# Moving the convolution and the transposes of block 1 one step later inside block 0

## The chip, the cores and the metric

The kernel runs on one core of a Trainium2 chip. The metric is device time in microseconds (us) of one execution. Traces come from the hardware profiler, one execution each. Engines: PE is TensorE, PEld its weight load, DVE is VectorE, ACT is ScalarE, POOL is GpSimd, SP issues DMAs.

## The reference, cut to what matters

```python
def _attn_ref(x, weight):                 # x: 8 x 4096 x 192, weight: 8 heads x 7 taps
    w = softmax(weight, axis=-1)          # (cut: written out, with 1e-9 in the sum)
    # causal convolution over the sequence, 7 taps, one set of taps for each head's 24 channels
    out = np.einsum('hk,bskhg->bshg', w, x_unf)
    return out.reshape(B, S, D)

def _moe_ref(x, w_gate, w_val, w_out):    # x: 32768 x 192, d_ff = 1536
    g = x @ w_gate
    silu = g * (1.0 / (1.0 + np.exp(-g)))
    val = x @ w_val
    return (silu * val @ w_out).astype(np.float32)
```

A short convolution feeds a gated feed-forward layer. The kernel works in blocks of 512 tokens (64 of them). A block has 12 chunks of 128 of the 1536 hidden columns, so there are 768 chunks in all, counted by `n` from 0.

## The kernel before: the parts that matter

For the first four blocks the convolution is made as small matmuls on PE (`early`), then turned by PE transposes (`eturn`; the fourth block by a DMA instead), then used by the chunks (`gate_val`). The results of PE go to banks of the memory PSUM; an eviction is the copy of a bank out of PSUM by ACT or DVE, after which the bank can be used again. A chunk is six matmuls, three pairs on the two row halves of the array. `slot(1, 0)` is the first accumulation of the output of block 0.

```python
# order of the loads on POOL's queue, at the start
xe_load(0)
...
load_w(0)                     # first two thirds of the gate and value weights
load_w(1)
xe_tile(1)
xe_load(1)                    # rows of block 1: two loads, one for each row half
load_w(2)                     # last third of the weights, needed from chunk 8 on
for m in range(3):
    load_wo(m)
...

def early(e, where):          # conv of block e: 64 small matmuls into three PSUM banks
    ...                       # moving operand: xe[e]
    # evictions: ACT (bank 0), DVE (bank 2), ACT (bank 1), then a DVE duplicate inside tme[e]

def eturn(b, where):          # transposes of block b: 3 x 5, each three into its own bank
    for k in range(SL):
        pool, tag = where[k]
        bank = pool.tile([P, EG, P], fp16, tag=tag, name="turn")
        ...                   # five PE transposes of tme[b] into bank
        (dve, act, dve)[k](...)    # eviction to xc: DVE, ACT, DVE

def gate_val(n):
    g = ppool.tile([P, TB], fp32, tag="gate", name="gate")    # three buffers each
    v = ppool.tile([P, TB], fp32, tag="val", name="val")
    ...                       # 3 pairs of matmuls
    silu[n] = seq(nc.scalar.activation(sg, g, AF.Silu)).ins
    seq(nc.vector.tensor_tensor(hj, sg, v, op=ALU.mult))      # the product of chunk n
    ...

acc_banks = (apool, "acc0"), (apool, "acc1")   # one buffer each: conv, transposes and
                                               # the accumulation share them
for n in range(n_steps):
    ...
    gate_val(n)
    if n == 5:
        early(1, (*acc_banks, gate_bank))
    elif n == 7:
        eturn(1, (*acc_banks, gate_bank))
    elif n in (9, 12, 15, 17):
        k = {9: 1, 12: 2, 15: 3, 17: 4}[n]
        slot(k, 0, silu[n - 1 if k == 4 else n - 2], work)
    ...
```

`seq` fixes the order of each engine's instructions as the program states it. The accumulation needs both accumulator banks, and the two row halves write both of them in turn, so it needs both of them empty.

Of the kernel before, what the change touches and what calls it, by code (L numbers as in the profile page):

```python
# [10 lines left out]
def kernel(  # L11
# [113 lines left out]
    def x16_tile(u):  # L125
        x16[u] = cpool.tile([P, 4 * NG, D], fp16, tag="x16", name="x16")
# [16 lines left out]
    def dup_x(u, queue=None):  # L143
        for r in range(2):
            p0 = Q * r
            seq(
                (queue or nc.sync).dma_start(
                    out=x16[u][p0 + 32 : p0 + 64], in_=x16[u][p0 : p0 + 32]
                )
            )  # L150
# [250 lines left out]
    def eout(e):  # L401
        scre[e] = dpool.tile([XW, 4 * Q], fp16, tag="scre", name="scre")
        rows = scre[e].rearrange("(g c j) d -> c j g d", c=2, j=EO)
        for c in range(2):
            seq(
                nc.sync.dma_start(
                    out=rows[c], in_=tme[e][Q * c : Q * c + EO, :, :]
                )
            )

    def efetch(b):
        xc[b] = []
        for k in range(SL):
            t = cpool.tile([P, XW], fp16, tag=f"xc{k}", name=f"xc{k}", bufs=6)
            seq(
                nc.sync.dma_start_transpose(
                    out=t[:, 0:TB], in_=scre[b][0:TB, Q * k : Q * k + P]
                )
            )
            xc[b].append(t)  # L420

    def eturn(b, where):
        xc[b] = []
        for k in range(SL):
            t = cpool.tile([P, XW], fp16, tag=f"xc{k}", name=f"xc{k}", bufs=6)
            pool, tag = where[k]
            bank = pool.tile([P, EG, P], fp16, tag=tag, name="turn")
            for g in range(EG):
                seq(
                    nc.tensor.transpose(  # L430
                        bank[:, g, :], tme[b][:, g, Q * k : Q * k + P], ident
                    )
                )
            seq(
                (dve, act, dve)[k](
                    t.rearrange("p (g c j) -> p g c j", c=2, j=EO),
                    bank.rearrange("p g (c q) -> p g c q", c=2)[:, :, :, 0:EO],
                )
            )
            xc[b].append(t)  # L440
# [47 lines left out]
    def conv_dup(u):  # L488
        seq(nc.gpsimd.tensor_copy(tm[u][:, :, SL * Q : 4 * Q], tm[u][:, :, 0:Q]))  # L489

    def conv_out(u, m):
        r, c = divmod(m, 4)
        t0 = NG * CO * m
        full = min(NG, (UT - t0) // CO)
        rest = min(UT - t0 - full * CO, CO) if full < NG else 0
        seq(
            nc.sync.dma_start(
                out=scr[u][t0 : t0 + full * CO, :].rearrange("(g j) d -> j g d", j=CO),
                in_=tm[u][32 * c : 32 * c + CO, NG * r : NG * r + full, :],
            )  # L500
        )
        if rest:
            t1 = t0 + full * CO
            seq(
                nc.sync.dma_start(
                    out=scr[u][t1 : t1 + rest, :],
                    in_=tm[u][32 * c : 32 * c + rest, NG * r + full, :],
                )
            )
# [3 lines left out]
    def fetch(b):  # L513
        u, i = divmod(b, UB)
        xc[b] = []
        for k in range(SL):
            t = cpool.tile([P, XW], fp16, tag=f"xc{k}", name=f"xc{k}", bufs=6)
            seq(
                nc.sync.dma_start_transpose(
                    out=t[:, 0:TB], in_=scr[u][TB * i : TB * i + TB, Q * k : Q * k + P]  # L520
                )
            )
            xc[b].append(t)
# [5 lines left out]
    def gate_val(n):  # L529
        b, j = divmod(n, NCH)  # L530
        g = ppool.tile([P, TB], fp32, tag="gate", name="gate")
        v = ppool.tile([P, TB], fp32, tag="val", name="val")
        m, e = divmod(j, E)
        for k in range(SL):
            for half, o in ((0, g), (1, v)):
                p0 = Q * half
                seq(
                    nc.tensor.matmul(  # L538
                        o,
                        w16[m][p0 : p0 + Q, k, e::E],  # L540
                        xc[b][k][p0 : p0 + Q, 0:TB],
                        start=(k == 0),
                        stop=(k == SL - 1),
                    )
                )
        sg = hpool.tile([P, TB], fp16, tag="sig", name="sig", bufs=3)
        silu[n] = seq(nc.scalar.activation(sg, g, AF.Silu)).ins  # L547
        hj = hpool.tile([P, TB], fp16, tag="h", name="h", bufs=15)
        seq(nc.vector.tensor_tensor(hj, sg, v, op=ALU.mult))  # L549
        hbuf[n] = hj  # L550
# [46 lines left out]
    def slot(k, b, after=None, between=None):  # L597

        if k == 1:
            acc[b] = [  # L600
                apool.tile([P, 2, D], fp32, tag=f"acc{i}", name=f"acc{i}")
                for i in range(2)
            ]
            down(b, [(False, G[0])], 1, after)
            if between is not None:
                between()
            down(b, [(False, G[1])], 1, None)
        elif k == 2:
            down(b, [(True, G[0]), (True, G[1])], 0, after)
            if between is not None:  # L610
                between()
            if b < n_blocks - 1:
                down(b, [(False, G[2])], 0, None)
        elif k == 3:
            down(b, [(True, G[2])], 1, after)
            if between is not None:
                between()
            down(b, [(False, G[3])], 1, None)
        else:
            down(b, [(True, G[3])], 0, after)  # L620
            o_sb = hpool.tile([P, SUBS, D], fp32, tag="o_sb", name="o_sb", bufs=3)
            seq(nc.scalar.copy(o_sb[:, 0:2, :], acc[b][0]))  # L622
            seq(nc.vector.tensor_copy(o_sb[:, 2:4, :], acc[b][1]))  # L623
            t0 = b * TB
            seq(
                nc.sync.dma_start(
                    out=out[t0 : t0 + TB, :].rearrange("(s p) d -> p s d", p=P),
                    in_=o_sb,
                )
            )  # L630
            del acc[b]
# [25 lines left out]
    for n in range(n_steps):  # L657
        b, j = divmod(n, NCH)
        u, ls = divmod(n, ustep)
        work = None  # L660
        if n in (12, 19):

            def work(e=2 if n == 12 else 3):
                early(e, (gate_bank, gate_bank, val_bank))

        at = (25, 31) if u == 0 else (10, 22)
        if u + 1 < NU and ls in at:

            def work(u=u, hh=at.index(ls)):
                conv_half(u + 1, hh)  # L670

        gate_val(n)
        if n == 5:
            early(1, (*acc_banks, gate_bank))
        elif n == 7:
            eturn(1, (*acc_banks, gate_bank))
        elif n in (9, 12, 15, 17):
            k = {9: 1, 12: 2, 15: 3, 17: 4}[n]
            slot(k, 0, silu[n - 1 if k == 4 else n - 2], work)
        elif j % 3 == 1 and n > 18:  # L680
            k = {1: 3, 4: 4, 7: 1, 10: 2}[j]
            slot(k, b - 1 if j < 7 else b, silu[n - 2], work)
        if n == 18:
            eturn(2, (*acc_banks, gate_bank))
        elif n == 20:
            eout(3)
        elif n == 21:
            efetch(3)
        if u + 1 < NU:
            if ls == at[0]:  # L690
                conv_dup(u + 1)
            if ls == at[1]:
                for m in range(2):
                    conv_out(u + 1, m)
            if ls == at[1] + 1:
                for m in range(2, 8):
                    conv_out(u + 1, m)
            lo = 32 if u == 0 else 28
            if ls in range(lo, lo + 12, 3):
                fetch(UB * (u + 1) + (ls - lo) // 3)  # L700
        if u + 2 < NU:
            if ls == (21 if u == 0 else 1):
                x16_tile(u + 2)
                load_x(u + 2, 0, silu[n - 1])
            if ls == (23 if u == 0 else 5):
                load_x(u + 2, 1, silu[n - 1])
            if ls == (37 if u == 0 else 26):
                dup_x(u + 2)
# [42 lines left out]
```

## Time and profile before

The median of three runs was 791.72 us (791.31 to 791.74). These are lines of the page of the kernel before: busy time of TensorE with its share of the span and its instructions, then the shares of the chain of work that ended last.

```profile
span 789.7 us, 28564 instructions
...
PE 782.5 (99%) x12007; PEld 526.3 (67%) x12007; DVE 583.0 (74%) x928; ACT 522.1 (66%) x910; POOL 67.6 (9%) x95
...
PE 97%; POOL 1%; DMA 1%; DVE 0%; ACT 0%; issue 0%; POOLq 0%
```

The chain of work is PE nearly everywhere, and the change removes no instruction, so it can only win time in which PE stands still. The DMA share of that chain (1%) is one load, `xe<-in_x_dram`. These are lines of the timeline of PE and of VectorE in the kernel before, from 12 to 20 us: start, length, engine, source line, operation, tiles, number of instructions, and in brackets idle time before with what ended it.

```profile
13.56 1.03 PE L372 MATMUL cv<-xe,wide 64*64 64x72 f16 x64 [0.43 <-DMA xe<-in_x_dram]
15.94 1.01 PE L430 MATMUL turn<-ident,tme 128*128 128x128 f16 x15
18.20 1.15 PE L564 MATMUL acc<-wo,h 64*128 64x192 f16 x24
...
16.02 1.34 DVE L549 TENSOR_TENSOR h<-sig,val 128x512 f16<-128x512 f16 x2 [0.22 <-PE val L538]
17.27 0.76 DVE L435 COPY xc<-turn 128x520 f16<-128x520 f16 x2
```

The three PE lines are the conv of block 1, its transposes and the first accumulation. The conv's first matmul is held by one load, and 63 of its matmuls are held by the other, which landed at 13.82 us. VectorE had emptied the first accumulator bank at 17.70, half a microsecond before the accumulation began at 18.20. The waits of the same kernel between 8 and 24 us (who waited for what: us in total, times, longest) name the load:

```profile
PEld L372 <- DMA xe<-in_x_dram: 0.7, 1, 0.7
...
PE cv L372 <- DMA xe<-in_x_dram: 0.4, 1, 0.4
```

### The profile page before, as it was taken

Reading aid. Unit: us, or ns where it says so; the run is one execution under the profiler, and the core shown is the slowest. Engines: PE = TensorE matmul, PEld = TensorE weight load, DVE = VectorE, ACT = ScalarE, POOL = GpSimd, SP = SyncE. Lnnn points to the kernel's source line nnn. Section 1 sums busy time; section 2 is a strip of 40 time slices with the busy share of each in tenths; the row PEclk is TensorE's granted clock in tenths of the full one; section 3 lists DMA queues with packets and bytes.
Section 4 is the critical chain, followed back from the end, with each engine's and each line's share of the span. In section 5 each row is a group of like instructions: output and inputs, shape, how many; then the busy total and the mean of one; then the engine's idle time right before and its main releaser. Section 6 shows DMA issues by size and latency. Waiting matters only on the chain.

```text
span 789.7 us, 28564 instructions
## 1 busy us (share of the span) xinstructions
PE 782.5 (99%) x12007; PEld 526.3 (67%) x12007; DVE 583.0 (74%) x928; ACT 522.1 (66%) x910; POOL 67.6 (9%) x95
## 2 busy tenths in 40 slices
PE   8999999999999999999999999999999999999997
PEld 4666666666666666666666666666666666666665
DVE  7677777777777777868777777777777777777775
ACT  6676666676666666666667666666667667676664
POOL 8201010010100101001010000100001010000000
PEclk9999999999999999999999999999999999999999
DMA  9999875797757868469794758857579784725311
GB/s 142 155 151 160 174 110 114 155 119 151 103 126 143 132 145 138 105 129 119 151 145 119 119 110 163 126 142 116 106 148 131 145 125 114 135 80 115 81 42 42
DMA packets 213825, 99.22 MB, mean 126 GB/s; under 512 B 147256, under 2 KB 212800, under 8 KB 212800
## 3 DMA queue, kind: packets, MB, share of 16 engines
q1 hardware_dynamic: 167696, 78.95, 48.2%
q0 software_dynamic: 46000, 18.45, 22.2%
q8 instruction: 94, 1.54, 0.8%
q14 instruction: 35, 0.29, 0.1%
HBM read 36.89 MB, written 41.16 MB: 99 GB/s over the span
## 4 chain that ended last, share of the span: by engine, by line
PE 97%; POOL 1%; DMA 1%; DVE 0%; ACT 0%; issue 0%; POOLq 0%
PE gate L538 61%; PE acc L564 32%; PE cv L461 2%; PE val L538 1%; DMA xe<-in_x_dram 1%; POOL w L167 0%; POOL xe L97 0%; PE acc L585 0%; PE cv L372 0%; PE turn L430 0%; DVE h L549 0%; ACT sig L547 0%; DVE o_sb L623 0%; ACT o_sb L719 0%; POOL jn L191 0%
## 5 line engine op out<-in xcount | busy, mean ns | idle before, releaser
L549 DVE TENSOR_TENSOR h<-sig,val 128x512 f16<-128x512 f16 x768 | 507.7, 688 | 194.8 <-PE val L538 191.6
L547 ACT ACTIVATE sig<-gate 128x512 f16<-128x512 f32 x768 | 458.5, 597 | 234.1 <-PE val L538 207.5
L538 PE MATMUL gate<-xc,w 64*128 64x512 f16 x2304 | 539.0, 376 | 0.0
L538 PE MATMUL val<-xc,w 64*128 64x512 f16 x2304 | 538.8, 376 | 0.1
L538 PEld LDWEIGHTS <-w 64*128 64x128 f16 x4608 | 253.7, 110 | 183.5 <-DMA w<-in_moe_w_val_dram 0.4
L564 PEld LDWEIGHTS <-h 64*128 64x128 f16 x6096 | 257.3, 94 | 62.4 <-issue 5.9
L564 PE MATMUL acc<-wo,h 64*128 64x192 f16 x6096 | 298.5, 243 | 0.0
L97 POOL DMA_DIRECT2D x<-in_x_dram x40 | 31.5, 794 | 435.8 <-ACT sig L547 427.1
L478 ACT CAST tm<-cv 128x480 f16<-128x480 f32 x60 | 30.6, 562 | 22.1 <-PE cv L461 22.1
L478 DVE CAST tm<-cv 128x480 f16<-128x480 f32 x60 | 36.6, 652 | 2.6
L623 DVE COPY o_sb<-acc 128x384 f32<-128x384 f32 x63 | 34.7, 551 | 0.0
L489 POOL COPY tm<-tm 128x1280 f16<-128x1280 f16 x15 | 18.8, 1252 | 136.3 <-DVE tm L478 128.1
L622 ACT COPY o_sb<-acc 128x384 f32<-128x384 f32 x63 | 30.2, 479 | 0.1
L461 PE MATMUL cv<-x,band 64*32 64x240 f16 x960 | 18.4, 265 | 0.0
L461 PEld LDWEIGHTS <-band 64*32 64x32 f16 x960 | 10.1, 91 | 5.0 <-issue 4.7
L132 POOL MEMSET x<- 6x192 f16 x7 | 1.7, 247 | 59.7 <-PE cv L461 59.6
L97 POOL DMA_DIRECT2D xe<-in_x_dram x9 | 6.0, 680 | 1.2 <-DMA xe<-in_x_dram 1.1
L639 PE MATMUL warm<-fill 128*128 128x512 f16 (+1 forms) x12 | 3.9, 483 | 1.0 <-DVE fill L91 1.0
L390 ACT CAST tme<-cv 128x288 f16<-128x288 f32 x8 | 2.9, 401 | 2.5 <-PE cv L372 2.5
L372 PE MATMUL cv<-xe,wide 64*64 64x48 f16 (+1 forms) x256 | 3.2, 192 | 1.1 <-ACT wide L330 0.6
L372 PEld LDWEIGHTS <-wide 64*64 64x64 f16 x256 | 2.7, 108 | 2.3 <-ACT wide L330 0.8
L430 PE MATMUL turn<-ident,tme 128*128 128x128 f16 x45 | 3.2, 220 | 0.6 <-ACT tme L390 0.5
(52 smaller groups left out, 37.2 us busy)
## 6 DMA issues: line engine op xcount, KB each, us to landing
out_dram<-o_sb SPq DMA_DIRECT2D x63, 384.0 KB
scr<-tm SPq DMA_DIRECT2D x105, 130.0 KB
x<-x SPq DMA_DIRECT2D x28, 480.0 KB
x<-in_x_dram POOLq DMA_DIRECT2D x24, 480.0 KB, 9.7
x<-in_x_dram POOLq DMA_DIRECT2D x7, 468.0 KB, 7.7
xc<-scr SPq DMA_TRANSPOSE x180
scr<-tm SPq DMA_DIRECT2D x15, 104.0 KB
w<-in_moe_w_gate_dram POOLq DMA_DIRECT2D x3, 192.0 KB, 5.3
```

Of the source, the lines that this page charges most:

```text
L97: nc.gpsimd.dma_start(out=t[p0 + i0 : p0 + i1, w0 - at : w1 - at, :], in_=bass.AP(tensor=x_flat.tensor, offset=(t0 + size * w0 - pad + i0) ...
L372: nc.tensor.matmul(o[Q * c : Q * c + Q, at : at + w], wide[Q * r : Q * r + Q, a, h, :], xe[e][Q * r : Q * r + Q, c : 2 * G : 2, h * grp : ...
L461: nc.tensor.matmul(banks[r][32 * c : 32 * c + 32, t * w : t * w + w], band[Q * r : Q * r + Q, h, :], x16[u][Q * r : Q * r + Q, NG * c : NG ...
L478: eng(tm[u][:, NG * r : NG * r + NG, 2 * grp * hp : 2 * grp * hp + 2 * grp].rearrange("p g (t e) -> p g t e", t=2), banks[r][:, 0 : 2 * w] ...
L489: seq(nc.gpsimd.tensor_copy(tm[u][:, :, SL * Q : 4 * Q], tm[u][:, :, 0:Q]))
L538: nc.tensor.matmul(o, w16[m][p0 : p0 + Q, k, e::E], xc[b][k][p0 : p0 + Q, 0:TB], start=(k == 0), stop=(k == SL - 1),)
L547: silu[n] = seq(nc.scalar.activation(sg, g, AF.Silu)).ins
L549: seq(nc.vector.tensor_tensor(hj, sg, v, op=ALU.mult))
L564: nc.tensor.matmul(acc[b][bank][:, s, :], hj[p0 : p0 + Q, ts(2 * bank + s, P)], wo16[p0 : p0 + Q, j, :], start=(not second and j == 0 and ...
L622: seq(nc.scalar.copy(o_sb[:, 0:2, :], acc[b][0]))
L623: seq(nc.vector.tensor_copy(o_sb[:, 2:4, :], acc[b][1]))
L639: nc.tensor.matmul(warm[:, 0:width], fill, fill.unsqueeze(1).to_broadcast([P, width // P, P]), start=True, stop=True, skip_group_check=True,)
```

## The change

The intent is to give the rows of block 1 one chunk (0.65 us) more to arrive, and to keep two chunks between the conv and its transposes, so that the conv's evictions have time.

```diff
         gate_val(n)
-        if n == 5:
+        if n == 6:
             early(1, (*acc_banks, gate_bank))
-        elif n == 7:
+        elif n == 8:
             eturn(1, (*acc_banks, gate_bank))
         elif n in (9, 12, 15, 17):
```

## The prediction

> **What bounds it now.** TensorE: busy 782.5 of 789.7 us on the page, and the chain of work that ended last is 97% PE. Busy time alone does not prove it (the Trainium skill, "Perfetto Trace Analysis", section "Identifying the Most-Contended Engine": matmul occupancy is not a good measure); the chain view does. So time is gained only where PE stands still, and the change touches only about 12.8 to 18.2 us.
>
> **The wait aimed at.** In the timeline the last pair of chunk 5 issues at 12.75 us (a pair takes 0.215). The conv of block 1 then waits for its input: two loads land at about 13.5 and 13.82 us, and 59 of its 64 matmuls are in the chain after 13.87. The next chunk starts at 14.52. The conv of block 2, unhindered, takes 0.66 us (22.22 to 22.89). So PE loses about 14.52 - 12.97 - 0.66 = 0.9 us.
>
> **What the change does.** No instruction is added or removed. Chunk 6 moves before the conv, chunk 8 before the transposes. Two chunks still lie between conv and transposes, but only chunk 9, not 8 and 9, between the transposes and the first accumulation of block 0. Estimates from these durations:
> 1. Chunk 6 (0.65 us) issues at 13.0 to 13.7; its banks come free at 12.93 (SiLU of chunk 3) and 13.00 (product of chunk 3). The conv starts near 13.7, waits until 13.87 for its second load, and ends at 14.52 as before. PE is one chunk, 0.65 us, ahead.
> 2. Chunks 7 and 8 issue from 14.52 to 15.85. Chunk 8 needs the last weight third, whose loads land at 14.57, 15.17 and 15.50 us: just in time.
> 3. Transposes at 15.93 to 16.85 as before; chunk 9 to about 17.55.
> 4. The accumulation wants both accumulator banks, which the transposes filled. VectorE empties the first only after its queue: product 6 (0.69, start 14.5), conv eviction (0.56), duplicate (0.45), products 7 and 8 (0.69 each), then 0.42. Estimated end 17.8 to 17.9, so PE waits 0.3 to 0.4 us there. Before, that eviction ended at 17.69 and the accumulation started at 18.20, without a wait.
>
> The Trainium skill, "TensorEngine Tiling (Array Packing)", section "PSUM Bottleneck", says tiling speeds up TensorE but not PSUM evacuation. The trace agrees here: a row-tiled chunk takes PE 0.65 us, VectorE's product 0.69.
>
> The accumulation thus starts near 17.95 instead of 18.20: of 0.65 us moved into the wait about 0.25 remains, the rest is given back at the accumulator banks. Later stages keep their order and are PE-bound.
>
> **Time.** 791.72 - 0.25 = 791.45 us; 791.0 to 791.95 should hold it 8 times in 10 (the runs before spread 0.43 us). Faster by over 2%: 0.003; within 2%: 0.994; slower: 0.003.
>
> **What the profile would show.** Right: PE's wait before the conv (timeline, waits) falls from 0.9 to at most 0.25 us; the conv's end stays near 14.5; a new PE gap of 0.2 to 0.5 us before the first accumulation, released by VectorE's eviction of the transposes; the accumulation starts at 17.8 to 18.05. Wrong: the conv ends at 13.9, no gap at the accumulation (gain 0.65), or it starts at 18.2 or later (gain zero or negative).
>
> **What would make it wrong.** Load landings that shift by some tenths: chunk 8 now meets its weights just as they land; a longer VectorE queue would take back the whole gain; run spread as large as the effect.

## The result, and the profile after

| kernel | runs | median us | lowest to highest us |
|---|---|---|---|
| before | 6 | 791.73 | 791.22 to 792.90 |
| changed | 6 | 791.55 | 791.16 to 792.59 |

The ratio is 0.9997, with a 95% interval of 0.9985 to 1.001. A ratio is the mean time of one kernel's runs over that of the other's of the same rounds, so it is not quite the ratio of the medians in the table. The interval is about 1 us to each side, so timing alone cannot show an effect of a few tenths; the traces have to.

These are the same timeline lines in the changed kernel.

```profile
14.05 0.73 PE L372 MATMUL cv<-xe,wide 64*64 64x72 f16 x64
16.13 1.01 PE L430 MATMUL turn<-ident,tme 128*128 128x128 f16 x15
17.75 1.34 PE L564 MATMUL acc<-wo,h 64*128 64x192 f16 x24
...
16.21 1.33 DVE L549 TENSOR_TENSOR h<-sig,val 128x512 f16<-128x512 f16 x2
17.46 0.76 DVE L435 COPY xc<-turn 128x520 f16<-128x520 f16 x2
```

The conv has no wait for its load. The accumulation begins 0.46 us earlier, but its 24 matmuls take 1.34 us instead of 1.15: the first is at 17.75, the second at 17.94, just after VectorE finished emptying the bank at 17.89. That is a pause of 0.19 us, which the kernel before does not have.

Taken chunk by chunk (start of each chunk's SiLU in the two traces), the changed kernel is 0.27 us earlier at chunk 13 and still 0.27 us earlier at chunk 767. So nothing after the first block takes up or adds to the difference of these two traces. But the first chunk was 0.25 us *later* in the changed kernel's trace, before the two programs differ at all. So the start-up has a draw of its own, and two traces are not enough.

### The profile page after: what moved, and what is told of

Same layout as the page of the kernel before. It is cut to its first block, busy times and chain, and to the rows that moved or that the text cites. A ratio compares the mean times of both kernels' runs of the same rounds, so it can differ in the third digit from the quotient of the medians. Undisturbed runs are those within 1.5% of the kernel's fastest.

```text
span 789.5 us, 28564 instructions
## 1 busy us (share of the span) xinstructions
PE 782.9 (99%) x12007; PEld 527.2 (67%) x12007; DVE 582.9 (74%) x928; ACT 522.1 (66%) x910; POOL 67.5 (9%) x95
## 4 chain that ended last, share of the span: by engine, by line
PE 99%; ACT 0%; DVE 0%; issue 0%
PE gate L538 62%; PE acc L564 32%; PE cv L461 2%; PE val L538 1%; PE warm L639 1%; PE turn L430 0%; PE cv L372 0%; PE acc L585 0%; ACT tme L390 0%; DVE h L549 0%; ACT wide L330 0%; ACT sig L547 0%; DVE o_sb L623 0%; ACT o_sb L719 0%; PE taps L317 0%
## 5 line engine op out<-in xcount | busy, mean ns | idle before, releaser
L430 PEld LDWEIGHTS <-tme 128*128 128x128 f16 x45 | 2.6, 97 | 1.8 <-issue 1.1
```

Of the source, the lines that this page charges most:

```text
L430: nc.tensor.transpose(bank[:, g, :], tme[b][:, g, Q * k : Q * k + P], ident)
```

## The experiments

Theory: the change removes up to one chunk (0.65 us) of a wait for the load of block 1's rows, whatever that wait is in a given run, and gives back a fixed pause at the accumulator banks, because only one chunk now lies between the transposes and the accumulation. Rivals: the difference of the two traces is chance at start-up; VectorE is the limit in this stage, so that time won at the load is lost to it; or the pause has another cause than the order of VectorE's work.

For each trace the table gives the start of the first chunk's SiLU (PE's own start-up), the landing of the second load of block 1's rows, the wait that the conv had for it (the time from the chunk before the conv to the chunk after it, less 0.215 us for the last pair, 0.66 for the conv and 0.09 that every trace has), the time from the first matmul of the chunk after the conv to the SiLU of chunk 13, and that from the SiLU of chunk 13 to that of chunk 767. All are read from single instructions of the traces, in us.

| trace | conv / transposes behind chunk | first SiLU | load lands | wait | after conv to chunk 13 | chunk 13 to 767 |
|---|---|---|---|---|---|---|
| before | 5 / 7 | 9.66 | 13.82 | 0.81 | 9.71 | 758.99 |
| rep_before | 5 / 7 | 10.13 | 13.64 | 0.15 | 9.71 | 759.37 |
| rep_before2 | 5 / 7 | 9.91 | 14.08 | 0.81 | 9.72 | 758.98 |
| before_nowait | 5 / 7 | 10.53 | 12.34, not used | 0 | 9.71 | 758.98 |
| before_late | 5 / 7 | 10.52 | 15.25 | 1.37 | 9.72 | 758.99 |
| changed | 6 / 8 | 9.91 | 13.93 | 0 | 9.25 | 758.99 |
| rep_after | 6 / 8 | 9.92 | 13.28 | 0 | 9.26 | 759.03 |
| rep_after2 | 6 / 8 | 9.91 | 13.31 | 0 | 9.26 | 758.98 |
| after_nowait | 6 / 8 | 9.73 | 13.77, not used | 0 | 9.25 | 759.01 |
| after_late | 6 / 8 | 9.96 | 15.69 | 1.63 | 9.25 | 759.91 |
| turn_only | 5 / 8 | 10.53 | 13.13 | 0 | 9.90 | 759.24 |
| conv_only | 6 / 7 | 9.69 | 13.18 | 0 | 9.23 | 760.60 |
| after_bank | 6 / 8 | 9.92 | 15.12 | 1.00 | 9.07 | 758.99 |
| after_first | 6 / 8 | 9.93 | 13.67 | 0 | 9.07 | 759.78 |

With the conv behind chunk 6 one chunk less is left to do after it. A chunk is three pairs of 0.2155 us, 0.65 us. If nothing were given back, the sixth column would read 9.71 - 0.65 = 9.06 to 9.07 us for these orders. The difference from that is the give-back.

### rep_before: the kernel before again

Edit: none.

> The kernel before again, unchanged, for a second trace of it. Main theory (PE loses about 0.9 us before the conv of block 1, to a load): the conv again waits for its second load, which lands at 13.8 give or take 0.2 us, whatever PE's own start-up does; first accumulation at 18.2 (18.0 to 18.4), without a wait for a bank. Rival (the 0.27 us between the two traces is the chance of two start-ups): the accumulation of this trace differs from the first trace of the same kernel by as much as 0.3 us.

The load landed at 13.64 and the accumulation began at 18.02, without a pause. But the conv waited only 0.15 us for it instead of 0.81, since PE had started 0.47 us later. Chunk 13 was 0.18 us earlier than in the first trace of the same program. So the theory's intervals hold, and the rival is right that single traces of one program differ by about as much as the effect.

### rep_after: the changed kernel again, timed

Edit: none beyond the change.

> The changed kernel again, unchanged. Main theory: conv ends at 14.5 to 14.75, its wait for the load is at most 0.2 us; first accumulation matmul at 17.55 to 17.8 and the second 0.1 to 0.3 us after it, when VectorE has emptied the bank; everything from chunk 13 on is 0.25 to 0.45 us earlier than in the kernel before, by the same amount to the end. Rival (chance): the shift is anywhere between -0.3 and +0.3. The timed ratio should be 0.9990 to 1.0005, too coarse to tell the two apart; the traces decide.

Accumulation at 17.76, its second matmul at 17.95: the pause repeats. The time after the conv repeats to 0.01 us. The shift at chunk 13 is -0.26 us against the first trace of the kernel before, but only -0.08 against rep_before: the expected 0.25 to 0.45 us does not hold for every pair. Timed: 791.45 us median (791.02 to 792.91, 6 runs) against 791.76 for the kernel before (11 runs), ratio 0.9997, 0.9985 to 1.0009.

### before_nowait: the old order without the load

```diff
-                                xe[e][
+                                xe[0 if e == 1 else e][
```

The result is wrong: block 1 is computed from block 0's rows.

> The kernel before, with the conv of block 1 reading the rows of block 0 (wrong result on purpose), which are there long before, so that it never waits for its load. Main theory: the conv ends at 13.6 to 13.9 and the whole 0.9 us is kept, since two chunks still lie between transposes and accumulation: first accumulation at 17.3 to 17.6, chunk 13 and all after 0.7 to 0.9 us earlier than in the kernel before. Rival (VectorE's queue is the limit here, and PE only waits elsewhere when the load comes early): accumulation at 17.8 or later with a wait for VectorE, gain 0.3 us or less.

The forecast of absolute times failed: the accumulation began at 18.27. The reason lies in the start-up, not at the conv: the first SiLU was at 10.53, 0.87 us later than in the first trace. The load landed at 12.34 here, so even the unedited kernel would not have waited in this execution. What this trace can still tell is the other half of the theory: the time from the conv to chunk 13 is 9.71 us as in the traces that waited, so time that is not spent on the wait is not lost to VectorE later in this order.

What drew the later start can be read in the timeline of the first microseconds. The first fence is the kernel before, the second before_nowait; the lines are PE's warming matmuls (eight, then four narrower ones) and the four matmuls that spread the taps.

```profile
1.00 3.28 PE L639 MATMUL warm<-fill 128*128 128x512 f16 x8 [1.00 <-DVE fill L91]
4.35 0.61 PE L639 MATMUL warm<-fill 128*128 128x256 f16 x4
5.01 0.60 PE L317 MATMUL taps<-spread,shift 128*128 128x256 f16 x4
```

```profile
1.00 3.59 PE L639 MATMUL warm<-fill 128*128 128x512 f16 x8 [1.00 <-DVE fill L91]
4.67 1.03 PE L639 MATMUL warm<-fill 128*128 128x256 f16 x4
5.50 1.06 PE L317 MATMUL taps<-spread,shift 128*128 128x256 f16 x4
```

The same four tap matmuls, whose inputs were ready in both, take 0.60 us in one and 1.06 in the other. Single ones took 269 to 272 ns against 421. The Trainium skill, "TensorE: Matmul & The Clock Gate", section "What's actually happening", says that PE starts at a slow clock and is let go after a busy window that runs freely, and that "the transition point varies ±500ns". The traces agree that the point varies, but it varies by more than that. PE's first matmul is at 1.00 us in all of them. In the first trace the matmuls turned fast during the seventh warming matmul, which ended at 4.07 us; in before_nowait the last tap matmul, begun at 6.14, was still slow. So the two points lie at least 2 us apart, and the traces' own record of the full clock begins at 3.84 and 6.72 us. The first SiLU varies over 0.88 us among the 14 traces. The landing of the load varies on its own, from 12.34 to 14.08 us in the traces with the old order and the loads in their place, and up to 15.12 (after_bank) with the new order.

### turn_only: only the transposes moved

```diff
-        elif n == 7:
+        elif n == 8:
             eturn(1, (*acc_banks, gate_bank))
```

> Half of the change: transposes behind the ninth chunk, conv left behind the sixth. Main theory: the wait for the load stays (conv ends at 14.5), and one chunk between transposes and accumulation is too few: VectorE's queue (products 6, 7, 8 after the conv's eviction) ends the eviction of the first bank about 18.4, so the second matmul of the accumulation waits 0.15 to 0.35 us, and chunk 13 and all after are 0.1 to 0.25 us later than in the kernel before. Rival (the give-back is no matter of VectorE's queue, only of the earlier PE): no wait at the accumulation, no shift.

The load landed early (13.13) and PE had started late, so the conv did not wait here; that part of the expectation fell. The pause came as expected, as the accumulation in the timeline shows: 24 matmuls take 1.34 us again.

```profile
18.28 1.34 PE L564 MATMUL acc<-wo,h 64*128 64x192 f16 x24
...
16.10 1.98 DVE L549 TENSOR_TENSOR h<-sig,val 128x512 f16<-128x512 f16 x3
18.00 0.76 DVE L435 COPY xc<-turn 128x520 f16<-128x520 f16 x2
```

From the conv to chunk 13 it takes 9.90 us instead of 9.71, so moving the transposes alone costs 0.19 us. The give-back belongs to the moved transposes, whether or not any wait for the load is removed.

### conv_only: only the conv moved

```diff
-        if n == 5:
+        if n == 6:
             early(1, (*acc_banks, gate_bank))
```

> The other half: conv behind the seventh chunk, transposes left behind the eighth, so one chunk between conv and transposes and two between transposes and accumulation. Main theory: the wait for the load goes (conv ends 14.5 to 14.75 with one chunk more done), but the transposes now wait 0.3 to 0.7 us for VectorE's eviction and duplicate of the conv (duplicate ends about 16.3), and the accumulation then waits for nothing: it starts at 17.8 to 18.1, 0.1 to 0.4 us earlier than in the kernel before. Rival (only the wait for the load matters, the evictions keep up): accumulation 0.6 us or more earlier.

The accumulation now has no pause (1.15 us, from 17.70), but the transposes wait. These are two lines of the waits between 13 and 18 us:

```profile
PEld L430 <- ACT tme L390: 0.4, 1, 0.4
...
PEld L430 <- DVE tme L390: 0.2, 1, 0.2
```

The transposes' own matmuls stretch over 0.96 us from the first start to the last instead of 0.79. The first line is no loss of its own: other traces have 0.4 us of the same weight load too, there put down to "issue". The second is new, the wait for VectorE's eviction of the conv. The total give-back is 9.23 - 9.06 = 0.17 us. I had expected 0.3 to 0.7 us at the transposes; it was less, and the accumulation began at 17.70 rather than 17.8 to 18.1. So the intent of the change, two chunks for the evictions, is worth little: either half order gives back nearly the same amount (0.17 or 0.19 us), once at the transposes, once at the accumulation.

### after_nowait: the new order without the load

The edit of before_nowait on the changed kernel, again with a wrong result.

> The changed kernel with the conv of block 1 reading the rows of block 0 (wrong result on purpose). Main theory: the changed order has hidden nearly all of the wait for the load already, so chunk 13 and all after come 0 to 0.15 us earlier than in the changed kernel. Rival (the changed kernel still loses time to the load): 0.3 us or more earlier.

The conv had no wait, as in the three unedited traces of the changed kernel, and the time from the conv to chunk 13 is the same 9.25 us. Chunk 13 comes 0.18 us earlier than in the first trace of the changed kernel, 0.03 us outside the expected 0.15, but the first SiLU was 0.18 us earlier too. So nothing of it is owed to the load.

### after_bank: another bank for the first transposes

```diff
         elif n == 8:
-            eturn(1, (*acc_banks, gate_bank))
+            eturn(1, (val_bank, acc_banks[1], gate_bank))
```

> The changed kernel with the first transposes of block 1 in a bank of the products' pool instead of the first accumulator, so that the accumulation no longer waits for VectorE's eviction, only for ScalarE's of the second accumulator. Main theory: the 0.19 us pause after the first accumulation matmul goes, chunk 13 and all after are 0.08 to 0.15 us earlier than in the changed kernel; chunk 9 or 10 may wait up to 0.1 us for a product bank and take that back. Rival (the pause comes from another cause, the weights of the accumulation or a SiLU): the pause stays at 0.15 us or more.

In this execution the load landed at 15.12, and the conv waited 1.00 us even behind chunk 6; so chunk 13 was not earlier than in the changed kernel but 0.93 us later. The pause did go: first and second matmul of the accumulation are both at 18.86, and the time from the conv to chunk 13 is 9.07 us, a give-back of zero. These are the lines of the accumulation and of VectorE's evictions in this trace:

```profile
18.86 1.16 PE L564 MATMUL acc<-wo,h 64*128 64x192 f16 x24
...
18.57 0.76 DVE L435 COPY xc<-turn 128x520 f16<-128x520 f16 x2
```

VectorE emptied the first transposes' bank only at 18.99, after the accumulation had begun. So the pause is a wait for that bank, not for weights or a SiLU.

### after_first: the bank is emptied before one product

```diff
         elif n == 8:
-            eturn(1, (*acc_banks, gate_bank))
+            eturn(1, (*acc_banks, gate_bank), held)
```

`gate_val(8)` holds its product back and returns it as `held`; `eturn` calls it after the eviction of its first bank. So VectorE's order is eviction, product of chunk 8, eviction, instead of product, eviction, eviction. Nothing else moves (the added source lines shift the line numbers of the profile).

> The changed kernel with one swap in VectorE's order: it evicts the first accumulator bank of the transposes before the product of chunk 8 instead of after. Main theory: the eviction ends at about 17.3 instead of 17.89, the accumulation's pause after its first matmul goes, and chunk 13 and all after are 0.08 to 0.15 us earlier than in the changed kernel, 0.35 to 0.5 us earlier than in the kernel before. Rival (another cause of the pause): pause stays. Timed ratio 0.9985 to 1.0005.

These are its lines of PE's accumulation and of VectorE:

```profile
17.76 1.15 PE L572 MATMUL acc<-wo,h 64*128 64x192 f16 x24
...
16.83 0.42 DVE L435 COPY xc<-turn 128x520 f16<-128x520 f16 x1
17.17 0.68 DVE L554 TENSOR_TENSOR h<-sig,val 128x512 f16<-128x512 f16 x1
17.77 0.42 DVE L435 COPY xc<-turn 128x520 f16<-128x520 f16 x1
```

The bank is empty at 17.26, the accumulation starts at the same 17.76 and takes 1.15 us: the pause is gone, and the give-back is zero. With nearly the same start-up (first SiLU 9.93 against 9.92 and 9.91), chunk 13 is at 23.80 against 23.98 and 23.97 in rep_after and rep_after2, so 0.17 to 0.18 us earlier. This is a little more than the 0.08 to 0.15 us that I had expected. Timed, it is not shown to be better: 791.84 us median (791.34 to 792.22, 5 runs) against 791.59 (9 runs), ratio 1.0001, interval 0.9987 to 1.0014. The 791.59 is the kernel before; no timed comparison with the changed kernel was made.

### before_late and after_late: the same late load in both orders

```diff
-xe_tile(1)
-xe_load(1)
 load_w(2)
+xe_tile(1)
+xe_load(1)
```

Both results are correct. This takes away the luck of the load: it is late in both.

> The kernel before with the load of block 1's rows issued after the last weight third instead of before it (result still correct), so that it lands late in every run: about 15.2 us (14.6 to 15.9) by the landings seen so far. Theory (what the change is worth is min(wait for that load, 0.65 us) less a fixed 0.13 us given back at the accumulator banks): the conv waits about 2 us (1.2 to 2.6) and starts when the load lands. This is the reference for the next run.

> The changed kernel with the same late load. Theory: the conv again starts when the load lands, but chunk 6 is already done; measured from the landing of the load, the first accumulation's end is 0.5 to 0.65 us earlier than in the run before_late, the give-back being 0 to 0.13 us. Rival (the change gains nothing, the two first traces differ by start-up alone): measured from the landing the accumulation ends at the same time, within 0.1 us.

The load landed at 15.25 in before_late and at 15.69 in after_late, and both convs waited for it (1.37 and 1.63 us; the first is at the low end of what was expected, since PE had started late). Measured from the landing, the chunk after the first accumulation begins after 5.37 us in the old order and after 4.85 in the new, 0.52 us earlier; chunk 13's SiLU comes after 10.41 and 9.95 us, 0.46 us earlier. That is 0.65 less 0.19, and not the rival's nothing. The theory had a give-back of at most 0.13 us and named the accumulation's end; by its last matmul the gain is 0.46 us too, just outside the expected 0.5 to 0.65. The 0.13 was read from the start of the chunk after the accumulation: the pause holds up one row half by 0.19 us and the other by about 0.13, and the two run 0.06 us out of step until chunk 13, where they are together again and the whole 0.19 us shows. The two times of these runs (793.01 and 793.82 us) do not show the gain: the load happened to land 0.45 us later in after_late, so chunk 13 is at nearly the same time in both (25.66 and 25.64), and PE then paused in that execution, as told below, so that the stretch to chunk 767 took 0.93 us longer.

after_late also tells what the pause is not. These are VectorE's lines from the conv's eviction to the emptying of the bank, and the accumulation:

```profile
19.43 1.34 PE L564 MATMUL acc<-wo,h 64*128 64x192 f16 x24
...
16.55 0.56 DVE L390 CAST tme<-cv 128x384 f16<-128x384 f32 x1 [1.21 <-PE cv L372]
17.21 0.30 DVE L399 COPY tme<-tme 128x320 f16<-128x320 f16 x1
17.89 1.33 DVE L549 TENSOR_TENSOR h<-sig,val 128x512 f16<-128x512 f16 x2 [0.37 <-PE val L538]
19.14 0.76 DVE L435 COPY xc<-turn 128x520 f16<-128x520 f16 x2
```

VectorE stood idle for 1.21 us and again for 0.37 us, so it had no backlog when the transposes came, and the pause is 0.19 us all the same. It is the position of one product ahead of the eviction, not the fill of the queue, that makes it; after_first showed the same by moving that one product.

### rep_before2 and rep_after2: a third draw of each

> The kernel before a third time, for another draw of the start-up and of the load. Theory: from the first chunk after the conv to the chunk after the first accumulation 4.67 us, as in its other traces; the wait for the load anywhere from 0 to 0.9 us, equal to the landing less the time PE was ready.

> The changed kernel a third time. Theory: from the first chunk after the conv to the chunk after the first accumulation 4.15 us (4.67 less one chunk of 0.65 plus 0.13 of pause at the accumulator banks); the wait for the load 0 to 0.3 us, unless the load lands after 14.1.

Both fall within what was expected: from the chunk after the conv to the chunk after the accumulation it took 4.67 and 4.16 us, the wait was 0.81 us in the old order and nothing in the new, and the pause came again (17.76, then 17.95). The first SiLU is at 9.91 us in both. Chunk 13 is at 24.50 and 23.97 us, but the load landed at 14.08 in one and at 13.31 in the other.

One more variant, the accumulation one chunk later, was not run: with the wait that it has, its matmuls of the two row halves would have written one bank without an order between them. It stays untested.

## Why the prediction was right or wrong

The forecast time (791.45 us, 791.0 to 791.95) holds the measured 791.55, and "within 2%" was right. This is no test of the mechanism: a loss of 0.19 us or a gain of 0.46 would have stayed in that range as well, and the six runs of the kernel before in the table above spread over 1.7 us. The view of the whole was right too: PE is what counts, only the first block is touched, and the shift reached in it stays to the end to a few hundredths where PE does not pause.

- **"So PE loses about ... 0.9 us".** Mis-sized, as a constant. In the trace at hand it was 0.81 us beyond the 0.09 that is always there. But the same program waited 0.15 and 0.81 us in its other two traces. In before_nowait and turn_only, which have the old order up to the conv, there was nothing to wait for. The wait is the difference of two draws, the landing of the load and PE's start at its full clock. One profile shows one draw.
- **"PE is one chunk, 0.65 us, ahead".** Right where the wait is at least that long: with the late load the new order was 0.65 less 0.19 us earlier.
- **Chunk 8 "just in time" for its weights.** Right; the last third landed at 14.67, 15.20 and 15.53 us in the trace after, and the chunk issued from 15.39 on without a gap.
- **"so PE waits 0.3 to 0.4 us there".** The wait and the bank were right; it came after the first matmul of the accumulation, not before it, and its size was 0.19 us, just under the forecast gap of 0.2 to 0.5. The eviction ended at 17.89 us, in the range forecast, but chunk 9 ended at about 17.75, not 17.55, since in that trace PE had started later and the conv ended at 14.71. The first matmul was at 17.75, before the forecast range of 17.8 to 18.05; the forecast of 17.95 was hit by the second (17.94), by two errors that cancelled, which is luck.
- **"VectorE empties the first only after its queue", from product 6 on.** The list of instructions was right, the reason too wide. Only the product of chunk 8, placed ahead of the eviction, matters.
- **"of 0.65 us moved into the wait about 0.25 remains".** For a run that waits 0.81 us, the runs give 0.65 - 0.19 = 0.46 us; for a run that doesn't wait, a loss of 0.19. An estimate for the average: from the start-up and the landing in the twelve traces without the late load, the old order would wait 0 to 1.65 us; the part up to 0.65 averages 0.33 us, and less 0.19 that leaves 0.14 us. This is too small for the timing here to show; the measured medians differ by 0.18 and 0.31 us, within intervals of about 1 us. So the net gain over many runs is an estimate; the two terms of it are shown.
- The Trainium skill's sentence on PSUM evacuation ("TensorEngine Tiling (Array Packing)", section "PSUM Bottleneck") fits the durations (0.69 us a product, 0.65 a chunk), but the cost found here was not one of throughput.

## What to carry to other kernels

The wait for a load at the start of this kernel was a draw (0 to 0.81 us in five traces of the old order), not a constant: before a step is moved to hide such a wait, it needs several traces. Measuring from an event (here the landing, or the chunk after the conv) to a later one made an effect of 0.2 us repeatable to 0.01 where whole times spread by over 1 us. When work moves later, look at what it now stands close to: here a shared bank made PE wait for the engine that empties it, and the order of two instructions on that engine decided whether it did. If the moved order is kept, emptying the bank before the product takes the 0.19 us back in the trace.

## What the Trainium skill lacked or had wrong

- "DMA: Bandwidth & Descriptors", section "Anatomy of one DMA — SWDGE (gpsimd) path", gives one DMA a fixed part of about 2 us and the bytes at 436 GB/s. By that (an estimate) the second load of block 1's rows, 96 KB, would take 2.2 us; with other loads in flight ahead of it, it took 4.6 (before_nowait) to 7.4 us (after_bank) from issue to landing. The page has no figure for how long one load takes behind others in its queue.
- "TensorE: Matmul & The Clock Gate", section "What's actually happening", is right that the transition to the fast clock varies, but its ±500 ns is too narrow for these traces: fast matmuls began by 4.07 us in one and after 6.14 in another. What it doesn't say is that a late start may cost nothing where a load is waited for afterwards: of the three traces of the kernel before, rep_before had the latest first SiLU (10.13) and still reached chunk 13 first (24.05 us, against 24.23 and 24.50); its load had landed first, too (13.64).
- "Perfetto Trace Analysis", section "Optimization Strategy", says to find the semaphore that a gap waits for. That section does not tell what to do with a gap that has none. From chunk 13 to 767 nine traces took 758.98 to 759.03 us and five took 759.24 to 760.60. In conv_only most of this was one pause in the middle of an accumulation, on instructions that wait for no semaphore, and the profile puts it down to "issue":

```profile
77.07 0.65 PE L564 MATMUL acc<-wo,h 64*128 64x192 f16 x11 [1.38 <-issue]
77.07 0.42 PEld L564 LDWEIGHTS <-h 64*128 64x128 f16 x10 [1.60 <-issue]
```

  rep_before, turn_only and after_late paused for less at the same place in PE's program; after_late and after_first paused at one more, near chunk 638. The two places are 17,664 PE instructions apart in the traces (give or take one), which is 69 times 256. The DMA queue whose kind the profile calls "instruction" (q8) brings 94 loads of 16 KB, one for about 256 of PE's 24,045 instructions, and in five of the six pauses PE went on 1.44 to 1.58 us after such a load had ended (2.86 in conv_only). So a late load of PE's own instructions is a candidate that no run tests. The cause stays open; the pause of conv_only alone is larger than the effect of this change.
- "TensorEngine Tiling (Array Packing)", section "PSUM Bottleneck", advises to use both ScalarE and VectorE for evacuation. It has nothing on the order within one of them: swapping one eviction and one product (after_first) removed the pause of 0.19 us.
